# Two decode layers on one core: a ring of 4 KB loads made one stretch of 28 KB, with larger loads and two regions exchanged

## The chip, the cores and the metric

One core of one Trainium2 chip runs the whole program. The metric is device time in microseconds for one execution, median of repeated runs: 707.14 us before the change, 706.82 to 707.31 over three runs. All data is float32, so the bytes that come from memory are fixed: about 299 MB in one execution.

## The reference

Two identical layers are applied to four rows of 512 numbers (a decode step for a batch of 4). Each layer is attention over a cache and then a gated feed-forward, both with a layer norm in front and a residual behind:

```python
x = x + attention(layernorm(x), k_cache, v_cache, wq, wo)   # 32 query heads, 8 groups, 4096 keys of 128
x = x + (silu(layernorm(x) @ w1) * (layernorm(x) @ w3)) @ w2  # 512 -> 1792 -> 512
```

Both layers use the same caches and the same weights. The caches of K and V are 67 MB each, the weights together 28 MB, far more than fits on the chip, so the second layer reads nearly everything again; only wq, wo and V of the last group stay between the layers.

## The kernel before, in words

**Units.** One tile, `arena`, holds all data that comes from memory. It has 216 units of 1 KB in each of the 128 partitions (128 KB over all partitions). Loads are counted in these units: a group's K or V is 64 units (8192 KB), a piece of a weight is 3 or 4 units (384 or 512 KB).

**The list of loads.** Lines 105 to 151 write out, by hand, the order of all 95 loads of the arena as `plan` entries: the source, the keys that a load brings, and for some a fixed place. `pump` (line 156) goes down this list whenever space has come free, takes a place from `take` (line 55), and issues the load from SyncE's queue at line 163. Since the list is in order, a load that has to wait holds all that stand behind it. What a load waits for on the chip is that the last reader of the units that it overwrites has read them. `done` and `vacate` give units back as the matmuls that read them are written.

**The first layer.** The regions are wq in 0 to 64, wo in 64 to 128, and `KEPT` in 128 to 192, where V of group 7 (`TURN`) stays for both layers. Until wo and that V come, the 128 units from 64 to 192 hold one group's K and one group's V in turn. Group 0's K is loaded in two halves, and group 7's V in four parts of 32, 16, 8 and 8 units. The scores (line 371) multiply a query against K blocks of 8 units; `weigh` (line 414) multiplies the weights of the softmax against V blocks of 8 units.

**The ring.** During the first feed-forward nothing else is free, so its weights and the first half of the second layer's first K pass through a ring of seven slots of 4 units: one at 64 to 68, where wo's first piece (key 0) was, which is saved to PSUM by `stash` and put back by `restore`, and six at 192 to 216. The last two units, 214 to 216, otherwise hold the softmax weights `pT`. `piece` (line 116) makes the loads of the ring: four each of w1a, w3a (4 units), w1b, w3b (3 units), seven of w2 and seven halves of K blocks (4 units). `product` (line 474) multiplies with one key of w1 or w3, `down` (line 496) with two keys of w2 by `pair` (line 433). `busy` (line 257) issues matmuls whose result nobody reads, between the others.

**The turn.** Behind the ring, the second layer's queries are made (line 315), and each use of a wq key gives 8 units back. The first loads after the ring go there: one more half block, four blocks of 8 units of K of group 7, and K of group 6 in parts of 8, 8, 8, 8, 16 and 16 units. From then on K and V come in loads of 32 and 64 units until the last feed-forward, whose weights are loaded in parts of 16, 12, 8, 4 and 2 units.

```python
for i in range(7):
    piece("half", i, slots[i])
ring["to"] = len(plan) - 1
piece("half", 7, None)
cache("k", 1, TURN, (8,) * (NB - SPLIT), SPLIT)
```

Of the kernel before, what the change touches and what calls it, by code (L numbers as in the profile page):

```python
# [15 lines left out]
REP = HQ // HKV  # L16
P = 128
KC = D // P
NB = 8
# [13 lines left out]
SPLIT = 4  # L33
# [4 lines left out]
def tile_decode_layers(ctx: ExitStack, tc: tile.TileContext, x, kt, v, wq, wo, w1, w3, w2, out):  # L38
# [9 lines left out]
    WQ, WO, KEPT = 0, 64, 128  # L48


    PT = ARENA - 2
    free = [(WO, PT - WO)]
    ring = {"to": 0}

    def take(n, at=None):
        if at is not None and at < WO:
            return at
        for i, (lo, size) in enumerate(free):
            if at is None and state["next"] > ring["to"]:

                end = min(lo + size, PT)
                if lo < WO + 4 and end > WO:
                    if WO - lo >= n:
                        end = WO
                    else:
                        lo = WO + 4
                if end - lo < n:
                    continue
                a = lo
                lo, size = free[i]  # L70
            else:
                a = lo if at is None else at
            if lo <= a and a + n <= lo + size:
                free[i:i + 1] = [(p, s) for p, s in ((lo, a - lo), (a + n, lo + size - a - n)) if s]
                return a
        return None
# [30 lines left out]
    for n in range(HKV):  # L107
        cache("k", 0, n, (32, 32) if n == 0 else (64,))
        if n == 0:
            load(wq[:, 8 * KB:64 * KB], 8, [("wq", 0, g) for g in range(1, HKV)], WQ + 8)  # L110
        else:
            cache("v", 0, n - 1, (64,))
    cache("v", 0, TURN, (32, 16, 8, 8))
    weights("wo", wo, 0, (32, 16, 8, 4, 4), 4, WO)

    def piece(name, i, at):

        w, layer, lo, n, per = {"w1a": (w1, 0, 4 * i, 4, 4), "w3a": (w3, 0, 4 * i, 4, 4),
                                "w1b": (w1, 0, 16 + 3 * i, 3, 3), "w3b": (w3, 0, 16 + 3 * i, 3, 3),
                                "w2": (w2, 0, 4 * i, 4, 2), "half": (kt[TURN], 1, 4 * i, 4, 4)}[name]  # L120
        weights(name, w[:, lo * KB:(lo + n) * KB], layer, (n,), per, at, 2 * i if name == "w2" else i)

    RING = KEPT + 64
    slots = [WO] + [RING + 4 * i for i in (5, 4, 3, 2, 1, 0)]
    for i in range(4):
        piece("w1a", i, (slots[6], slots[1], slots[2], slots[3])[i])
    for i in range(4):
        piece("w3a", i, (slots[4], slots[5], slots[0], slots[6])[i])
    for i in range(4):
        piece("w1b", i, RING + 21 - 3 * i)  # L130
    for i in range(2):
        piece("w3b", i, RING + 9 - 3 * i)
    piece("w2", 0, slots[0])
    for i in range(2, 4):
        piece("w3b", i, RING + 9 - 3 * i)
    for i in range(1, 7):
        piece("w2", i, slots[i])
    for i in range(7):
        piece("half", i, slots[i])
# [16 lines left out]
    def pump():  # L156
        while state["next"] < len(plan):
# [7 lines left out]
            if i == 0:  # L165
                nc.sync.dma_start(xt[:8], x[:8])
# [23 lines left out]
    nc.scalar.dma_start(xt[8:], x[8:])  # L190
# [242 lines left out]
    def pair(i, left, w, first, last):  # L433

        for n in range(2):
            for e in range(2):
                r = 32 * (2 * n + (e ^ (i % 2)))
                nc.tensor.matmul(x_ps[r:r + B, e * 256:e * 256 + 256], left(2 * i + n), w(n)[:, e * 256:e * 256 + 256],
                                 start=first, stop=last)
# [11 lines left out]
    def restore():  # L451
        assert take(4, WO) == WO
# [3 lines left out]
    def project_o(layer, g, first=False, last=False):  # L456
        for i in range(2):
# [3 lines left out]
            if last or not layer and g == TURN - 1:  # L461
                pair(i, lambda h: oT[:, g, h, :], lambda j: w[:, j, :], False, last and i == 1)
# [7 lines left out]
    def feed_forward(layer, mean):  # L470
# [3 lines left out]
        def product(name, ps, lo, n, fill=keep, ks=range(KC)):  # L474
            for k in ks:
# [20 lines left out]
        def down(i):  # L496
            ws = [loaded("w2", layer, 2 * i + n) for n in range(2)]
            if keep:
                pair(i, lambda m: hT[:, m, :], lambda n: ws[n], i == 0, i == WT // 2 - 1)
            else:  # L500
                for n in range(2):
                    for k in range(KC):
                        nc.tensor.matmul(x_ps[32 * k:32 * k + B, 0:P], hT[:, 2 * i + n, :],  # L503
                                         ws[n][:, k * P:(k + 1) * P], start=False, stop=(i == WT // 2 - 1 and n == 1))
            for n in range(2):
                done("w2", layer, 2 * i + n)
# [130 lines left out]
```

## Time and profile before

| | before |
|---|---|
| median of 3 runs | 707.14 us |
| the profiled execution itself | 706.78 us |
| its span, first to last instruction | 705.0 us |
| PE busy | 400.1 us, 57% |
| DVE busy | 85.0 us, 12% |
| ACT busy | 38.3 us, 5% |
| SyncE's DMA queue, share of 16 engines | 99.1% |
| read from memory | 298.85 MB |
| loads into the arena | 95 |

The page comes from one execution. Shares of the span are averages over stages. The row of DMA digits gives the busy share of the 16 DMA engines in 40 slices of the span, and the row under it what they moved. A chain of waits, followed back from the last instruction, shows which work ended last at each step. The profiled execution took 1.78 us more than its span, for what lies around the first and last instruction, and 0.36 us less than the median.

### The profile page before, as it was taken

Reading aid. Unit: us, or ns where it says so; the run is one execution under the profiler, and the core shown is the slowest. Engines: PE = TensorE matmul, PEld = TensorE weight load, DVE = VectorE, ACT = ScalarE, POOL = GpSimd, SP = SyncE. Lnnn points to the kernel's source line nnn. Section 1 sums busy time; section 2 is a strip of 40 time slices with the busy share of each in tenths; the row PEclk is TensorE's granted clock in tenths of the full one; section 3 lists DMA queues with packets and bytes.
Section 4 is the critical chain, followed back from the end, with each engine's and each line's share of the span. In section 5 each row is a group of like instructions: output and inputs, shape, how many; then the busy total and the mean of one; then the engine's idle time right before and its main releaser. Section 6 shows DMA issues by size and latency. Waiting matters only on the chain. (4 is left out here: it accounts for less than half of the span.)

```text
span 705.0 us, 6895 instructions
## 1 busy us (share of the span) xinstructions
PE 400.1 (57%) x3082; PEld 132.1 (19%) x3082; DVE 85.0 (12%) x290; ACT 38.3 (5%) x87; POOL 2.9 (0%) x10
## 2 busy tenths in 40 slices
PE   4555454546555553547677894365563545467666
PEld 2111011111111120112143231011120111122224
DVE  2001010101011010101111111020010101010111
ACT  0000000000000000002001000000000000000101
POOL 0000000000000000000000000000000000000000
PEclk9766777777677787768899997587697878788899
DMA  9999999999999999999999999999999999999996
GB/s 387 461 403 472 414 417 436 450 417 431 455 416 432 435 436 420 442 421 423 413 404 406 416 438 438 446 424 421 461 421 424 440 439 421 431 432 419 426 425 270
DMA packets 14003, 299.35 MB, mean 425 GB/s; under 512 B 1687, under 2 KB 1815, under 8 KB 6551
## 3 DMA queue, kind: packets, MB, share of 16 engines
q1 hardware_dynamic: 13840, 298.92, 99.1%
q8 instruction: 24, 0.39, 0.2%
q10 hardware_dynamic: 135, 0.01, 0.0%
q14 instruction: 4, 0.03, 0.0%
HBM read 298.85 MB, written 0.07 MB: 424 GB/s over the span
## 5 line engine op out<-in xcount | busy, mean ns | idle before, releaser
L414 PE MATMUL o_ps<-arena 128*32 128x512 f32 x1024 | 145.7, 718 | 150.8 <-DMA arena<-in_v 137.6
L371 PE MATMUL s_ps<-arena,qpad 128*32 128x512 f32 x1024 | 152.1, 749 | 82.5 <-DMA arena<-in_kt 82.5
L414 PEld LDWEIGHTS o_ps<-arena 128*32 128x32 f32 x1024 | 37.3, 129 | 257.3 <-issue 224.5
L371 PEld LDWEIGHTS s_ps<-arena,qpad 128*32 128x32 f32 x1024 | 39.5, 133 | 177.7 <-issue 165.6
L423 DVE SCALAR_TENSOR_TENSOR p<-o_ps,parts,p 128x512 f32<-128x512 f32 x16 | 12.0, 750 | 270.9 <-PE o_ps L414 270.9
L378 DVE TENSOR_REDUCE top<-s_ps 128x1 f32<-128x512 f32 x16 | 11.0, 690 | 194.0 <-PE s_ps L371 194.0
L315 PE MATMUL o_ps<-arena,xpad 128*32 128x512 f32 x112 | 16.2, 707 | 10.5 <-DMA arena<-in_wq 10.5
L421 ACT ACTIVATE p<-o_ps,parts 128x512 f32<-128x512 f32 x16 | 11.0, 687 | 192.5 <-PE o_ps L414 184.6
L445 PE MATMUL x_ps<-arena,oT 128*4 128x512 f32 x104 | 14.1, 653 | 9.1 <-DMA arena<-in_wo 5.6
L402 PE MATMUL t_ps<-ident,p 128*128 128x128 f32 x64 | 11.2, 302 | 13.5 <-ACT p L396 13.5
L425 PE MATMUL t_ps<-ident,p 128*128 128x128 f32 x64 | 10.5, 287 | 14.3 <-DVE p L423 14.2
L389 ACT ACTIVATE f<-d 128x1 f32<-128x1 f32 x16 | 3.2, 203 | 256.3 <-DVE d L387 256.3
L396 ACT ACTIVATE p<-s_ps,top 128x512 f32<-128x512 f32 x16 | 10.9, 684 | 75.9 <-PE t_ps L425 75.9
L425 PEld LDWEIGHTS t_ps<-ident,p 128*128 128x128 f32 x64 | 6.7, 141 | 29.6 <-DVE p L423 29.6
L403 DVE COPY arena<-t_ps 128x512 f32<-128x512 f32 x16 | 11.1, 691 | 9.6 <-PE t_ps L402 9.6
L259 PE MATMUL m_ps<-ident,rows 128*32 128x128 f32 x70 | 11.9, 273 | 0.0
L402 PEld LDWEIGHTS t_ps<-ident,p 128*128 128x128 f32 x64 | 7.1, 147 | 22.2 <-ACT p L396 19.2
L478 PE MATMUL o_ps<-arena,xpad 128*32 128x192 f32 (+1 forms) x128 | 8.1, 360 | 2.9 <-DMA arena<-in_w 2.8
L478 PE MATMUL s_ps<-arena,xpad 128*32 128x192 f32 (+1 forms) x128 | 7.9, 359 | 2.3 <-DMA arena<-in_w 2.1
L259 PEld LDWEIGHTS m_ps<-ident,rows 128*32 128x32 f32 x70 | 7.5, 110 | 3.5
L315 PEld LDWEIGHTS o_ps<-arena,xpad 128*32 128x32 f32 x112 | 3.7, 126 | 20.7 <-DMA arena<-in_wq 11.6
L320 DVE COPY p<-o_ps 128x256 f32<-128x256 f32 x2 | 0.8, 424 | 44.9 <-PE o_ps L315 44.9
(97 smaller groups left out, 139.9 us busy)
## 6 DMA issues: line engine op xcount, KB each, us to landing
arena<-in_kt SPq DMA_DIRECT2D x4, 4096.0 KB, 20.1
arena<-in_v SPq DMA_DIRECT2D x4, 4096.0 KB, 33.0
arena<-in_w SPq DMA_DIRECT2D x17, 512.0 KB, 10.1
arena<-in_kt SPq DMA_DIRECT2D x8, 1024.0 KB, 9.8
arena<-in_wq SPq DMA_DIRECT2D x1, 7168.0 KB, 39.5
arena<-in_v SPq DMA_DIRECT2D x3, 2048.0 KB, 36.8
arena<-in_wo SPq DMA_DIRECT2D x1, 4096.0 KB, 25.5
arena<-in_kt SPq DMA_DIRECT2D x8, 512.0 KB, 8.2
```

Source lines behind the costliest of these rows:

```text
L259: nc.tensor.matmul(m_ps[turn["m"] ^ 1][0:32, 384:512], rows, ident, start=True, stop=True)
L315: nc.tensor.matmul(ps[32 * k:32 * k + 32, :], xpad[:, k, lo:lo + 32], w[:, k, :], start=first, stop=last)
L371: nc.tensor.matmul(s_ps[32 * b:32 * b + 32, :], qpad[:, b, lo:lo + 32], k[:, j, :], start=(blk == 0), stop=(blk == NB - 1))
L378: nc.vector.tensor_reduce(top[:, 0:1], s_ps, axis=AX.X, op=ALU.max, negate=True)
L402: nc.tensor.transpose(t_ps[:, i, :], p[:, i * P:(i + 1) * P], ident)
L403: nc.vector.tensor_copy(pT.rearrange("p i r -> p (i r)"), t_ps.rearrange("p i r -> p (i r)"))
L414: nc.tensor.matmul(o_ps[32 * b:32 * b + 32, :], pT[:, i, 32 * b:32 * b + 32], w[:, b, :], start=(i == 0), stop=(i == NI - 1))
L421: nc.scalar.activation(p, o_ps, AF.Copy, scale=st["parts"][:, 0:1])
L423: nc.vector.scalar_tensor_tensor(p, o_ps, st["parts"][:, 1:2], p, op0=ALU.mult, op1=ALU.add)
L425: nc.tensor.transpose(t_ps[:, j, :], p[:, j * P:(j + 1) * P], ident)
L445: nc.tensor.matmul(x_ps[r:r + B, :], left(2 * i + n), w(n), start=first, stop=False)
L478: nc.tensor.matmul(ps[32 * j:32 * j + 32, lo:lo + n], x32[:, k, :], w[:, j * n:(j + 1) * n], start=(k == 0), stop=(k == KC - 1))
```

## The change

The list of loads has 77 entries instead of 95. The regions KEPT and WO exchange places: KEPT is 64 to 128, WO 128 to 192. wo is laid out from the top down, with key 0 at the end of the first load, so that key 0's four units lie at 188 to 192 and join the units 192 to 216 to one ring of 28 units. The loads of the ring have 4, 6 or 8 units and lie at any offset in it. Three blocks of the second layer's first K come as halves (`SPLIT`), not four, as loads of 8, 4, 4, 4 and 4 units; behind the ring come 8, 16 and 16 units, and K of group 6 comes in four loads of 16. K of group 0 comes as one load of 64 units, V of group 7 as two of 32. `take` keeps new loads off the four units of wo's key 0 in the second layer, as before. `down` takes one key of w2 at a time (`half_product` issues half of `pair`'s matmuls), and no product with w2 stands between those with w3b any more. All 128 rows of x are loaded from ScalarE's queue, where 8 of them came from SyncE's. The order of wo's heads in memory changes to fit.

```diff
-SPLIT = 4
+SPLIT = 3
-    WQ, WO, KEPT = 0, 64, 128
+    WQ, KEPT, WO = 0, 64, 128
-    PT = ARENA - 2
-    free = [(WO, PT - WO)]
+    PT, RING = ARENA - 2, WO + 60
+    free = [(KEPT, PT - KEPT)]
...
+            at = WO if (which, layer, g) == ("k", 0, 0) else at
...
-        cache("k", 0, n, (32, 32) if n == 0 else (64,))
+        cache("k", 0, n, (64,))
...
-    cache("v", 0, TURN, (32, 16, 8, 8))
-    weights("wo", wo, 0, (32, 16, 8, 4, 4), 4, WO)
-    def piece(name, i, at):
...
+    cache("v", 0, TURN, (32, 32))
+    lo = 64
+    for first, n in ((None, 32), (8, 16), (12, 8), (14, 4), (15, 4)):
+        lo -= n
+        some = [*range(1, 8), 0] if first is None else range(first, first + n // 4)
+        r = 0 if first is None else 4 * first
+        load(wo[:, r * KB:(r + n) * KB], 4, [("wo", 0, i) for i in some], WO + lo)
+    for name, r, n, per, first, at in (
+            ("w1a", 0, 4, 4, 0, 4), ("w1a", 4, 4, 4, 1, 8), ("w1a", 8, 8, 4, 2, 12), ("w3a", 0, 8, 4, 0, 20),
+            ("w3a", 8, 4, 4, 2, 0), ("w3a", 12, 4, 4, 3, 4), ("w1b", 16, 6, 3, 0, 8), ("w1b", 22, 6, 3, 2, 14),
+            ("w3b", 16, 6, 3, 0, 20), ("w3b", 22, 6, 3, 2, 0), ("w2", 0, 8, 2, 0, 6), ("w2", 8, 6, 2, 4, 14),
+            ("w2", 14, 8, 2, 7, 20), ("w2", 22, 6, 2, 11, 0), ("half", 0, 8, 4, 0, 6), ("half", 8, 4, 4, 2, 14),
+            ("half", 12, 4, 4, 3, 18), ("half", 16, 4, 4, 4, 22), ("half", 20, 4, 4, 5, 0)):
+        w = {"w1": w1, "w3": w3, "w2": w2, "ha": kt[TURN]}[name[:2]]
+        weights(name, w[:, r * KB:(r + n) * KB], int(name == "half"), (n,), per, RING + at, first)
     ring["to"] = len(plan) - 1
-    piece("half", 7, None)
-    cache("k", 1, TURN, (8,) * (NB - SPLIT), SPLIT)
+    cache("k", 1, TURN, (8, 16, 16), SPLIT)
     for n in range(1, HKV):
-        cache("k", 1, order[1][n], {1: (8, 8, 8, 8, 16, 16), 2: (32, 32)}.get(n, (64,)))
+        cache("k", 1, order[1][n], {1: (16, 16, 16, 16), 2: (32, 32)}.get(n, (64,)))
...
-            if i == 0:
-                nc.sync.dma_start(xt[:8], x[:8])
...
-    nc.scalar.dma_start(xt[8:], x[8:])
+    nc.scalar.dma_start(xt, x)
...
-        product("w3b", o_ps, FA, FB, ks=range(0, 2))
-        if keep:
-            down(0)
-        product("w3b", o_ps, FA, FB, ks=range(2, KC))
+        product("w3b", o_ps, FA, FB)
...
-        for i in range(1 if keep else 0, WT // 2):
-            if i == (4 if keep else 0):
+        for m in range(WT):
+            if m == (8 if keep else 0):
                 tail_tiles()
-            down(i)
+            down(m)
```

## Rows read from the trace of the kernel before

**Rows 1.** The page: span, engines, DMA queues.

```profile
span 705.0 us, 6895 instructions
PE 400.1 (57%) x3082; PEld 132.1 (19%) x3082; DVE 85.0 (12%) x290; ACT 38.3 (5%) x87; POOL 2.9 (0%) x10
...
q1 hardware_dynamic: 13840, 298.92, 99.1%
q8 instruction: 24, 0.39, 0.2%
```

**Rows 2.** The chain that ended last, in order: start us, us, what.

```profile
446.82 33.26 DMA arena<-in_kt
...
488.67 30.10 DMA arena<-in_kt
...
526.80 32.19 DMA arena<-in_kt
...
567.38 30.31 DMA arena<-in_kt
...
701.37 0.45 PE x_ps L503 x8
```

**Rows 3.** Two stretches: us, busy by engine, granted clock, DMA share, GB/s.

```profile
350.00:400.00 50.00, 42.00 (x449) 18.92 (x445) 6.03 (x28) 4.07 (x10) 1.10 (x2) 1.00 1.02 407
430.00:440.00 10.00, 6.16 (x32) 1.50 (x32) 0.00 (x0) 0.00 (x0) 0.00 (x0) 0.66 1.02 437
```

**Rows 4.** Line 163, three single loads: start; the line below, us to landing.

```profile
L163 SPq DMA_DIRECT2D arena<-in_kt x1: 328/328/328, 376.4 to 376.4; - x1
DMA to landing us min/median/max: 8.2/8.2/8.2
...
L163 SPq DMA_DIRECT2D arena<-in_kt x1: 328/328/328, 386.0 to 386.0; - x1
DMA to landing us min/median/max: 6.2/6.2/6.2
...
L163 SPq DMA_DIRECT2D arena<-in_kt x1: 328/328/328, 395.8 to 395.8; - x1
DMA to landing us min/median/max: 16.3/16.3/16.3
```

**Rows 5.** PE in order of time, two starts on 3-unit loads: start, us, what.

```profile
367.36 0.53 PE L478 MATMUL s_ps<-arena,xpad 128*32 128x192 f32 x8 [0.18 <-DMA arena<-in_w]
...
369.29 0.53 PE L478 MATMUL s_ps<-arena,xpad 128*32 128x192 f32 x8 [0.22 <-DMA arena<-in_w]
```

**Rows 6.** PE in order of time, around the other merged loads.

```profile
24.99 6.45 PE L371 MATMUL s_ps<-arena,qpad 128*32 128x512 f32 x32 [3.48 <-DMA arena<-in_kt]
41.93 9.09 PE L315 MATMUL o_ps<-arena,xpad 128*32 128x512 f32 x56 [10.49 <-DMA arena<-in_wq]
...
320.40 3.64 PE L414 MATMUL o_ps<-arena 128*32 128x512 f32 x32 [0.86 <-ACT p L421]
...
334.34 3.64 PE L414 MATMUL o_ps<-arena 128*32 128x512 f32 x32 [1.21 <-ACT p L421]
...
345.17 1.88 PE L445 MATMUL x_ps<-arena,oT 128*4 128x512 f32 x7 [5.59 <-DMA arena<-in_wo]
```

**Rows 7.** PE in order of time, from the ring's end to the turn.

```profile
379.03 0.33 PE L538 MATMUL t_ps<-ident,p 128*128 128x128 f32 x1
...
379.91 0.61 PE L438 MATMUL x_ps<-arena,qT 128*4 128x256 f32 x8 [0.28 <-DVE qT L494]
...
380.85 0.61 PE L438 MATMUL x_ps<-arena,qT 128*4 128x256 f32 x8
...
382.13 0.61 PE L438 MATMUL x_ps<-arena,qT 128*4 128x256 f32 x8 [0.46 <-DMA arena<-in_w]
...
384.91 1.06 PE L315 MATMUL t_ps<-arena,xpad 128*32 128x512 f32 x8
```

**Rows 8.** Line 163, the first load of all: start; the line below, us to landing.

```profile
L163 SPq DMA_DIRECT2D arena<-in_wq x1: 368/368/368, 0.7 to 0.7; - x1
DMA to landing us min/median/max: 4.8/4.8/4.8
```

More of the change, by code (lines that the diff above doesn't have):

```diff
@@ L45, in tile_decode_layers @@
     arena = const.tile([P, ARENA * KB], F32, name="arena")
-    WQ, WO, KEPT = 0, 64, 128
-    PT = ARENA - 2
-    free = [(WO, PT - WO)]
+    WQ, KEPT, WO = 0, 64, 128
+    PT, RING = ARENA - 2, WO + 60
+    free = [(KEPT, PT - KEPT)]
     ring = {"to": 0}
     def take(n, at=None):
-        if at is not None and at < WO:
+        if at is not None and at < KEPT:
             return at
+        closed = state["next"] > ring["to"] and at is None
         for i, (lo, size) in enumerate(free):
[L59 to L75, printed above, removed]
+            parts = [(lo, RING), (RING + 4, PT)] if closed else [(lo, lo + size)]
+            for a, end in parts:
+                a, end = max(a, lo), min(end, lo + size)
+                a = a if at is None else at
+                if lo <= a and a + n <= end:
+                    free[i:i + 1] = [(p, s) for p, s in ((lo, a - lo), (a + n, lo + size - a - n)) if s]
+                    return a
         return None
@@ L431, in weigh, with half_product @@
         nc.vector.tensor_tensor(oT[:, g].rearrange("p h b -> p (h b)"), raw, st["r"], op=ALU.mult)
[L433 to L439, printed above, removed]
+    def half_product(m, left, w, first, last):
+        for e in range(2):
+            r = 32 * (2 * (m % 2) + (e ^ (m // 2 % 2)))
+            nc.tensor.matmul(x_ps[r:r + B, e * 256:e * 256 + 256], left, w[:, e * 256:e * 256 + 256], start=first, stop=last)
     def whole(i, left, w, first):
@@ L461, in project_o @@
             if last or not layer and g == TURN - 1:
-                pair(i, lambda h: oT[:, g, h, :], lambda j: w[:, j, :], False, last and i == 1)
+                for j in range(2):
+                    half_product(2 * i + j, oT[:, g, 2 * i + j, :], w[:, j, :], False, last and i == 1)
             else:
@@ L494, in tiles, with down @@
             nc.vector.tensor_copy(hT[:, 4 * lo:4 * lo + n, :], t_ps.rearrange("p i (j b) -> p (i j) b", j=4)[:, 4 * lo:4 * lo + n, 0:B])
-        def down(i):
-            ws = [loaded("w2", layer, 2 * i + n) for n in range(2)]
+        def down(m):
+            w = loaded("w2", layer, m)
             if keep:
-                pair(i, lambda m: hT[:, m, :], lambda n: ws[n], i == 0, i == WT // 2 - 1)
+                half_product(m, hT[:, m, :], w, m < 2, m >= WT - 2)
             else:
[L501 to L506, printed above, removed]
-            if keep and i < WT // 2 - 1:
+                for k in range(KC):
+                    nc.tensor.matmul(x_ps[32 * k:32 * k + B, 0:P], hT[:, m, :], w[:, k * P:(k + 1) * P],
+                                     start=False, stop=(m == WT - 1))
+            done("w2", layer, m)
+            if keep and m % 2 and m < WT - 1:
                 busy()
-            elif not keep and i in (1, 3):
+            elif not keep and m in (3, 7):
                 busy(3)
```

30 lines of the change are left out of this document (5 added, 25 removed).

## The prediction

> **What bounds the kernel now.** I read the page first, for who is busy, then the chain, for what ended last, then stretches and single loads, for what one load costs. On the page [rows 1] SyncE's DMA queue fills 99.1% of the 16 DMA engines' time, while PE is busy for 57% and no other engine for over 12%. The chain [rows 2] agrees: from 446 us on it alternates between a K load in flight and the few matmuls that free the space for a load after it, and each piece marked DMA spans 30 us because the load queued behind others, not because it is slow. So the end of the program is the end of a stream of loads that hardly ever pauses, plus PE's last 0.45 us and the store. The time can change in three ways only: the stream needs less time for the same bytes, the stream runs dry somewhere, or the tail behind the last byte changes. The last six loads, which feed the tail, keep their sizes and order, so I cost the tail at nothing.
>
> Is the stream equally fast everywhere? No [rows 3]: it moved 407 GB/s from 350 to 400 us, where loads of 3 and 4 units pass, and 437 GB/s from 430 to 440 us, where they have 32 units or more, at a DMA share of 1.02 in both. The engines are equally full, but small loads carry something besides bytes.
>
> **What one load costs besides its bytes.** Landings that follow one another in a full queue give the time per load. K loads of 64 units: the chain [rows 2] has landings at 480.08 (446.82 + 33.26), 518.77, 558.99 and 597.69, with a V load between each two, so a load takes 38.69 / 2 = 19.35 us, and again 38.70 / 2. Loads of 8 units: from 392.2 to 412.1 [rows 4] eight of them land, 2.49 us each. Loads of 4 units: from 384.6 to 392.2 there are six, 1.27 us each. Loads of 3 units: PE starts on them 1.93 us apart for two, 0.965 us each [rows 5]. Now the same 64 units by each size: 8 x 2.49 = 19.9 us, 0.55 us over 19.35 for 7 more loads, 0.08 each; 16 x 1.27 = 20.3 us, 0.95 for 15 more, 0.06 each; 21.3 x 0.965 = 20.6 us, 1.23 for 20.3 more, 0.06 each. A load in a full queue costs 0.06 to 0.08 us besides its bytes.
>
> **The change part by part.** It removes 18 loads: 1 of K of group 0, 2 of V of group 7, 1 each of w1a and w3a, 2 each of w1b and w3b, 3 of w2, 4 of the halves and K of group 7, 2 of K of group 6. 18 x 0.06 = 1.1 us, 18 x 0.08 = 1.4 us; I take 0.067, nearer to the small sizes where most of them are, so 1.2 us. As I find no row where the stream of the first layer or of the ring stands still, all of it lies on the path.
>
> The 18 issues that SyncE saves, 0.33 us each [rows 4], are worth nothing: the queue holds five and more microseconds of work at each. PE does the same matmuls, since `half_product` twice is `pair`.
>
> K of group 0 in one load: its first matmul starts where the second half's do now, at 24.99 us, and the whole needs twice the 6.45 us of a half, until 38 us. PE's next step waits for wq until 41.93 us [rows 6], so this hides, with 4 us to spare; and without that cover V of group 0 would still come in time, since K of group 1 takes the stream 19 us beyond wq. x from one queue: 8 rows move from SyncE's queue to ScalarE's, 0 to 0.1 us, and PE has nothing to do with q before 24.99 us; nothing.
>
> V of group 7 in two loads: PE starts its second half at 334.34 us, while the last parts are still coming, and is through at 337.98; later it waits 5.59 us for wo [rows 6]. Even a start at 337.98 us, when the last part must long have landed, delays it by 3.64 us only, inside that wait. wo's first load, which lands at about 345 us, will wait until PE has read all of group 6's V, at 324.04 (320.40 + 3.64), 21 us ahead of its landing and with V of group 7 queued in front of it: nothing.
>
> **The ring's new waits** are the term that can go wrong. A load of 8 units waits for two keys that have themselves come in one load, so each space comes free later, in steps of 2.5 us. I followed each load to the last reader of the units it overwrites and put landings at the new times. Within the ring each is issued 4 to 6 us ahead of its predecessor's landing; today that is 5 at the narrowest (386.0 us against 392.2 less 1.27 [rows 4]).
>
> The narrowest is the first load behind the ring, block 3 of K of group 7 (8 units), which waits for PE to read wq's first key of the second layer. That PE step comes after all of w2. Its predecessor, the last half block, lands at 389.7 us now (392.2 less two loads of 4) and will at 388.9, with 0.8 us saved by then. Before that come halves of 8, 4, 4, 4 and 4 units (7.6 us) and w2's last load of 6 (1.88 us, between 1.27 and 2.49), so w2's last three keys land at 381.3 us and the four before them at 379.4. PE then takes key 7 (0.3 us), the tiles (379.03 to 379.91 now, 0.88 us [rows 7]) and three pairs 0.94 us apart (379.91 to 380.85), and is done with w2 at 383.2 us, against 382.74 now. That is 0.45 us later; the chain from there to wq's first key keeps its length, and the issue goes from 386.0 to 386.45 us. The lead shrinks from 5.0 to 2.4 us. Behind it on SyncE's queue stand the two loads of 16 units of K of group 7; they wait for further wq keys, their leads come out a little wider by the same working, and PE's scores wait for all three.
>
> Which lead is needed, no row shows, since no load is ever issued so late. Bounds: the first load of all lands 4.8 us after its issue [rows 8] and needs 2.49 for its bytes, so 2.3 us of fixed time; what part of that lies behind the last byte, the predecessor's landing has too. So the lead needed is between 0 and 2.3 us, and 2.4 just clears the upper end. I cost it at nothing; if the sum of PE steps is 0.5 us longer than mine and the upper bound holds, it costs 0.4 us there and about as much at the next load.
>
> Behind the turn, scores of group 6 wait for 16 units at a time. The loads that then depend on them are issued well over 5 us ahead, and PE has less left when the last 16 units come than the 9.7 us that the next 32 take: nothing.
>
> **Sum.** 706.78 - 1.2 = 705.6 us for the profiled execution; it stood 0.36 us under the median of the runs, so 705.9 us against 707.14. That is 0.17% less, and a measurement of this kernel can tell about 0.2%, 1.4 us: the forecast is a small gain that counts as no change.
>
> **The rivals.**
> *The gain is larger.* At 0.08 us a load it is 1.44 us, 705.7. There is also a pause that I leave as it is: from 518.77 to 558.99 us the two loads took 40.22 and not 38.70 us [rows 2], 1.5 us more, and 24 packets of instructions go over the same engines [rows 1]. If one such pause fewer falls on the engine that is last, 704.4. For it: these costs add on the same engines. Against: the instruction count hardly changes.
>
> *Nothing is left of it.* The leads at the turn fall short by up to a microsecond at two loads, or the 0.06 us is not paid on the slowest engine: 706.2 to 708.5 us.
>
> *Slower: PE turns slow in the ring and the queue runs dry at the turn.* Today PE works at full clock through the ring (1.00 from 350 to 400 us, busy for 42 of 50 us, small waits between), while between 430 and 440 us, busy for 6.2 of 10 us on large loads, 0.66 is granted [rows 3]. With loads of 8 units PE gets its work in larger lumps with longer waits between. If the clock falls to the lower of its two levels (1.2 GHz) there, the 3.8 us of PE work from 382.13 to 385.97 us [rows 7] become about 7. The issue then comes at 389.6 us, 0.7 us after the predecessor's landing; with half of the upper bound needed as lead it is dry for 1.8 us, and the two loads behind lose about as much again each, as their wq steps slow too: 3.6 to 5.4 us lost, less 1.2, so 709.5 to 711.3. It decides from 2.6 us lost on. Against it: the fillers of `busy` stay in place and the waits in the ring grow only to about 1.2 us (2.49 less two products of 0.6). The Trainium skill, "TensorE: Matmul & The Clock Gate", section "HAM oscillation", speaks against the change here: a loop whose compute per tile is shorter than the wait for the next tile's DMA goes back to the low clock at every tile. By that rule this rival would be the likeliest; the row of 350 to 400 us, with a wait for DMA at every load and a clock of 1.00, does not bear it out so far.
>
> *A load's fixed time is paid in series.* The first load's 2.3 us [rows 8], 18 times, would be 41 us: 666 us. The 1.27 us between landings of 4 units [rows 4] exclude it nearly. The Trainium skill, "DMA: Bandwidth & Descriptors", section on the anatomy of one DMA, gives each DMA about 2.0 us of fixed cost, measured on GpSimd's path; an estimate from that page would be 36 us less, and the trace does not agree.
>
> **How the numbers follow.** The forecast, a gain of 0.9 to 1.4 us, gets 0.48; the larger gain 0.30; nothing left 0.10; slower through the clock 0.11; in series 0.01. Faster by over 0.2% is 0.31, within 0.2% is 0.58, slower 0.11. The range reaches down to 705.0, for most of the larger gain, and up to 707.9, for most of the case where nothing is left; the slow rival lies outside.
>
> **What would show it.** Right: 77 loads, fewer small packets, the 350 to 400 us stretch above 410 GB/s, landings of 6 units about 1.88 us apart, the load at the turn issued about 386.4 us with a lead over 2 us, and the same 38.7 us per pair afterwards, each some 1.2 us earlier. Wrong: a granted clock under 1.00 between 355 and 390 us, a landing interval over 3 us for the 8 units at the turn, or landings of K at 64 units no earlier than now.

## The result, and the profile after

| | before, same chip | after |
|---|---|---|
| median | 706.98 us (10 runs) | 708.48 us (10 runs) |
| lowest to highest | 706.68 to 707.31 | 707.24 to 712.05 |
| the profiled execution, its span | | 712.05 us, 710.3 us |

The kernel became slower: the ratio is 1.0029, interval 1.0018 to 1.0039. Not only the median moved: the times lie 4.8 us apart where those of before lie 0.6 apart. That narrow spread is partly luck of ten runs: in the longer series below the kernel before reaches 709 us too. The profiled execution was the slowest of the ten, so its losses are larger than the median's; what it shows is where time can be lost.

The page of the kernel after (span, engines, DMA queues), beside [rows 1]:

```profile
span 710.3 us, 6864 instructions
...
PE 405.0 (57%) x3082; PEld 137.8 (19%) x3082; DVE 85.3 (12%) x290; ACT 38.4 (5%) x87; POOL 2.9 (0%) x10
...
q1 hardware_dynamic: 11232, 298.91, 98.3%
```

There are 2,608 packets fewer for the same bytes, as the change says, but the queue is 98.3% full and no longer 99.1%: somewhere it stood empty. PE is busy 4.9 us longer with the same 3082 matmuls, so its clock was lower somewhere. Two stretches account for this. The first is the ring and the turn. Windows of the kernel after (us, busy PE, PEld, DVE, ACT, POOL with counts, granted clock, DMA share, GB/s), beside [rows 3]:

```profile
360.00:366.00 6.00, 6.00 (x48) 3.28 (x49) 0.98 (x5) 0.47 (x1) 0.55 (x1) 0.50 0.94 355
366.00:372.00 6.00, 4.70 (x72) 3.12 (x71) 1.00 (x3) 1.91 (x3) 0.00 (x0) 0.97 0.94 324
372.00:376.00 4.00, 1.85 (x31) 1.04 (x22) 0.42 (x1) 0.00 (x0) 0.00 (x0) 1.00 1.00 415
376.00:380.00 4.00, 3.65 (x33) 1.88 (x34) 0.00 (x0) 0.00 (x0) 0.00 (x0) 0.57 1.00 420
...
350.00:400.00 50.00, 43.73 (x445) 20.77 (x437) 6.13 (x28) 4.08 (x10) 1.10 (x2) 0.90 1.00 391
```

The first two of these stretches in the kernel before:

```profile
360.00:366.00 6.00, 4.29 (x52) 2.19 (x52) 0.89 (x5) 0.47 (x1) 0.56 (x1) 1.00 1.03 401
366.00:372.00 6.00, 4.90 (x68) 2.49 (x62) 1.00 (x3) 1.91 (x3) 0.00 (x0) 1.00 1.03 398
```

From 350 to 400 us 391 GB/s moved, where it was 407. Most of the loss lies between 360 and 372 us, and the clock stood at its lower level (1.2 GHz) for six microseconds just there, and again from 376 us. Four loads of the ring and the turn in the kernel after (the load's line is 146: start, and under it us to landing):

```profile
L146 SPq DMA_DIRECT2D arena<-in_w x1: 328/328/328, 365.1 to 365.1; - x1
...
DMA to landing us min/median/max: 6.1/6.1/6.1
...
L146 SPq DMA_DIRECT2D arena<-in_w x1: 328/328/328, 367.1 to 367.1; - x1
...
DMA to landing us min/median/max: 6.6/6.6/6.6
...
L146 SPq DMA_DIRECT2D arena<-in_kt x1: 328/328/328, 379.8 to 379.8; - x1
...
DMA to landing us min/median/max: 7.3/7.3/7.3
...
L146 SPq DMA_DIRECT2D arena<-in_kt x1: 328/328/328, 389.5 to 389.5; - x1
...
DMA to landing us min/median/max: 9.0/9.0/9.0
```

The two loads of w3b (6 units) landed at 371.2 and 373.7 us, 2.5 us apart, where 6 units take 1.88 in a full queue. I call such an excess a load's **lateness**: the time between two landings, less 0.06 us and 0.302 us for each unit (19.35 us for 64). The **lead** is how long before its predecessor's landing a load is issued. In this execution w1b's second load was late by 0.17 us, w3b's two (leads 3.7 and 4.2) by 0.60 and 0.59, the half block of 4 units issued at 379.8 (lead 5.1, behind a load with 3.9) by 0.87, and the first load of 16 units, issued at 389.5, by 0.17: 2.4 us. In the kernel before no load of the ring or the turn was late by more than 0.10.

PE in order of time, in the kernel after, shows where the clock fell:

```profile
357.71 1.07 PE L458 MATMUL s_ps<-arena,xpad 128*32 128x256 f32 x16
359.93 1.93 PE L458 MATMUL s_ps<-arena,xpad 128*32 128x256 f32 x16 [1.14 <-DMA arena<-in_w]
...
362.74 1.08 PE L458 MATMUL o_ps<-arena,xpad 128*32 128x256 f32 x8
```

Sixteen matmuls take 1.07 us at 357.71, and behind a wait of 1.14 us for a load of 8 units eight take 1.08.

The second stretch is the tail. From the chain that ended last, and from PE in order of time, both in the kernel after:

```profile
590.19 27.67 DMA arena<-in_v
...
631.56 46.28 DMA arena<-in_v
677.88 3.69 PE o_ps L395 x16
...
706.12 1.37 PE x_ps L482 x43
```

```profile
677.88 3.64 PE L395 MATMUL o_ps<-arena 128*32 128x512 f32 x16 [4.37 <-DMA arena<-in_v]
...
689.20 3.64 PE L458 MATMUL s_ps<-arena,xpad 128*32 128x256 f32 x32 [0.26 <-DVE xpad L282]
...
693.72 3.64 PE L458 MATMUL o_ps<-arena,xpad 128*32 128x256 f32 x32
```

The first of these products in the kernel before:

```profile
684.06 1.93 PE L478 MATMUL s_ps<-arena,xpad 128*32 128x256 f32 x32 [0.26 <-DVE xpad L301]
```

In [rows 2] the chain ends with a DMA and 0.45 us of PE. Here it leaves the DMA for good at 677.88; from there it is PE's, with short steps of DVE between. A product of 32 matmuls takes 3.64 us (1.93 in the kernel before) until about 697: behind the wait of 4.37 us for V the clock stayed low, with PE hardly idle. PE was late when the last bytes came. They came at 703.66 us (701.33 before), and the span ended 6.6 us later (3.7 before). So the 5.3 us more of this execution are **2.3 in the stream and 2.9 in the tail**.

The stream's 2.3 can be added up: 18 loads fewer, -1.1; lateness in ring and turn, +2.4; +1.3 because outside the ring four landings came about 1.4 us late (at 62.7, 335.2, 424.2 and 677.8 us), where the kernel before has three of that kind (62.7, 330.4 and 539.6); small deviations make up the rest, -0.3.

### The profile page after: what moved, and what is told of

Same layout as the page of the kernel before. It is cut to its first block, busy times and chain, and to the rows that moved or that the text cites. A ratio compares the mean times of both kernels' runs of the same rounds, so it can differ in the third digit from the quotient of the medians.

```text
span 710.3 us, 6864 instructions
## 1 busy us (share of the span) xinstructions
PE 405.0 (57%) x3082; PEld 137.8 (19%) x3082; DVE 85.3 (12%) x290; ACT 38.4 (5%) x87; POOL 2.9 (0%) x10
## 3 DMA queue, kind: packets, MB, share of 16 engines
q1 hardware_dynamic: 11232, 298.91, 98.3%
## 5 line engine op out<-in xcount | busy, mean ns | idle before, releaser
L395 PE MATMUL o_ps<-arena 128*32 128x512 f32 x1024 | 149.1, 732 | 152.2 <-DMA arena<-in_v 140.4
L352 PE MATMUL s_ps<-arena,qpad 128*32 128x512 f32 x1024 | 146.6, 728 | 89.7 <-DMA arena<-in_kt 89.7
L458 PE MATMUL o_ps<-arena,xpad 128*32 128x192 f32 (+1 forms) x128 | 11.6, 470 | 2.0 <-DMA arena<-in_w 2.0
L458 PE MATMUL s_ps<-arena,xpad 128*32 128x192 f32 (+1 forms) x128 | 10.6, 455 | 1.9 <-DMA arena<-in_w 1.6
L418 PE MATMUL x_ps<-arena,qT 128*4 128x256 f32 x56 | 6.7, 479 | 1.7 <-DMA arena<-in_w 1.3
```

The source lines that it names most:

```text
L352: nc.tensor.matmul(s_ps[32 * b:32 * b + 32, :], qpad[:, b, lo:lo + 32], k[:, j, :], start=(blk == 0), stop=(blk == NB - 1))
L395: nc.tensor.matmul(o_ps[32 * b:32 * b + 32, :], pT[:, i, 32 * b:32 * b + 32], w[:, b, :], start=(i == 0), stop=(i == NI - 1))
L458: nc.tensor.matmul(ps[32 * j:32 * j + 32, lo:lo + n], x32[:, k, :], w[:, j * n:(j + 1) * n], start=(k == 0), stop=(k == KC - 1))
```

## The experiments

Four theories stood at the start or came up later. **Clock** (A): PE's clock falls in the ring, the products take longer, the loads are issued too late. **Leads** (B and D): the larger loads wait for more work to be done, are issued later, and at any clock this is too late; D says why a lead of 2 to 4 us is too late, namely that the 16 DMA engines do not run dry together: the landing counts the last of them, so some are empty while the predecessor is still landing. **Tail** (C): the end comes late because the clock is low in the tail, whatever the stream does. Each run stands against the kernel before on the same chip: the first four kernels below share one series, the next four a second, the last three and the second execution of six halves a third. The intervals of the ratios reach some 0.7 us to either side. Only three of the experiments lie clear of the kernel before, all slower: fillers in the tail, seven halves, and large ring with small turn. The argument therefore leans on the landings in the profiled executions, one of each kernel and two of the changed one.

**The same kernel again.** No edit.

> The changed kernel once more, nothing edited. Theory A (PE's clock falls to its lower level in the ring, PE reads late, SyncE issues late, the DMA engines that are ahead run dry): about 708.5 us, 1.5 above the kernel before, single times spread over 707 to 712; the profile has a granted clock under 0.9 between 355 and 385 us and loads of 6 units more than 2.1 us apart, and the more of the one the more of the other. Theory B (leads in the ring are too short at any clock, or rows of 6 KB are slow in themselves): the same median, but slow landings of 6 units also where the clock is 1.00. Theory C (PE's clock falls in the last feed-forward, and the end comes up to 3 us after the last landing): the profile has 4 us or more from the last landing to the end of the span where the clock is low after 677 us, and 3.7 where it is not.

Measured: 707.82 us (706.52 to 710.91), before 707.1, ratio 1.0011 [0.9999, 1.0022]. The loss is smaller than the first time and no longer clear of noise, with the same wide spread. In this execution the clock stood at 1.00 from 360 to 372 us, and w3b's second load was late all the same, by 0.65, and at the turn the 8 units (lead 2.8) by 0.31, the first 16 (lead 3.4) by 0.84. The last byte landed at 702.2 us and the tail took 3.3: the tail is not what makes the usual execution slow. Rows of 6 KB are not slow in themselves, as B also had it: two loads of 6 units in the kernel after, with leads of 6.3 and 5.7 us, landed 1.89 and 1.88 us behind their predecessors.

**More fillers in the ring.** `busy`, the matmuls that nobody reads, issues three where a merged load ends, not one.

```diff
-                    busy()
+                    busy(3 if k % 2 and keep else 1)
+                elif keep and k == 1:
+                    busy(3)
...
-            if keep and m % 2 and m < WT - 1:
+            if keep and m in (3, 6, 10):
+                busy(2)
+            elif keep and m % 2 and m < WT - 1:
```

> The changed kernel with more fillers of PE in the first feed-forward, 3 for 1 at the end of each load and 3 after w1a's second key, so that PE has no long idle stretch there; no load is touched. Theory A: clock 1.00 from 350 to 395 us, loads of 6 units 1.88 and of 8 units 2.49 us apart, 1.0 to 2.5 us less than the changed kernel: 706.0 to 707.5. Theory B: the clock rises, the landings stay 2.1 to 2.5 us apart for 6 units, 708.5. Theory C alone: 708.5 with the whole excess behind the last landing.

Measured: 707.95 us (707.36 to 708.60), 1.0008 [0.9999, 1.0017]. The slowest executions are gone, and the quickest too. Windows, and three loads, of this kernel:

```profile
366.00:372.00 6.00, 4.97 (x71) 3.75 (x72) 0.61 (x2) 1.91 (x3) 0.00 (x0) 1.00 1.01 405
...
386.00:387.00 1.00, 1.00 (x14) 0.46 (x10) 0.39 (x2) 0.00 (x0) 0.00 (x0) 1.00 0.97 393
387.00:388.00 1.00, 1.00 (x12) 0.26 (x8) 0.28 (x4) 0.37 (x1) 0.51 (x1) 1.00 0.77 246
388.00:389.00 1.00, 1.00 (x11) 0.35 (x4) 0.24 (x1) 0.00 (x0) 0.04 (x1) 1.00 0.94 320
389.00:390.00 1.00, 1.00 (x11) 0.78 (x14) 0.17 (x1) 0.00 (x0) 0.00 (x0) 1.00 1.01 426
```

```profile
L146 SPq DMA_DIRECT2D arena<-in_kt x1: 332/332/332, 383.3 to 383.3; - x1
...
DMA to landing us min/median/max: 5.7/5.7/5.7
...
L146 SPq DMA_DIRECT2D arena<-in_kt x1: 328/328/328, 386.6 to 386.6; - x1
...
DMA to landing us min/median/max: 5.3/5.3/5.3
...
L146 SPq DMA_DIRECT2D arena<-in_kt x1: 328/328/328, 388.8 to 388.8; - x1
...
DMA to landing us min/median/max: 9.0/9.0/9.0
```

The last half block landed at 383.3 + 5.7 = 389.0 us, yet from 387 to 388 only 246 GB/s moved and the engines were 0.77 full: many had nothing left, a microsecond or two before that landing. The trace counts 16 completions for each load, and the last of them is its landing. Ten of this half block's lie between 387.2 and 387.9 us. The first of the 8 units' comes at 390.9, so their bytes, 2.48 us of them, began to move at about 388.4: ten engines were empty for 0.5 us and more. The 8 units were issued at 386.6, with a lead of 2.4, and were late by 0.35; the 16 units (388.8 + 9.0) were late by 1.01. All this at a clock of 1.00 from 366 us on; ahead of that the fillers had not held it (0.76 from 355 to 360 us). So the clock is not needed for the loss, and what D claims of the engines is seen.

**A ring of small loads.** The ring's 19 loads become 30 of 2 to 4 units; regions and turn stay (88 loads).

```diff
-            ("w1a", 0, 4, 4, 0, 4), ("w1a", 4, 4, 4, 1, 8), ("w1a", 8, 8, 4, 2, 12), ("w3a", 0, 8, 4, 0, 20),
+            ("w1a", 0, 4, 4, 0, 4), ("w1a", 4, 4, 4, 1, 8), ("w1a", 8, 4, 4, 2, 12), ("w1a", 12, 4, 4, 3, 16),
+            ("w3a", 0, 4, 4, 0, 20), ("w3a", 4, 4, 4, 1, 24), ("w3a", 8, 4, 4, 2, 0), ("w3a", 12, 4, 4, 3, 4),
...
```

> The changed kernel with the loads of the ring cut again to 2, 3 and 4 units, 88 loads, in the one stretch; the exchanged regions, the larger loads in front of the ring and behind it stay. Theories A and B both: the ring runs as before, landings 1.27 and 0.98 us apart, 7 loads fewer than before give 0.4 to 0.5 us: 706.5 against 707.0. If instead the loads at the turn lose the time: still 708 to 708.5. Theory C alone: 708 and the same spread as the changed kernel.

Measured: 706.69 us (706.31 to 708.52), 0.9996 [0.9987, 1.0005]. No load of the ring was late by over 0.15 us; at the turn one was, the first 16 units (lead 4.0) by 0.47. Against 707.82 us for the changed kernel in the same series the ring's loads had cost about a microsecond, though the single times overlap (706.52 to 710.91 and 706.31 to 708.52).

**Fillers in the tail.** `busy(8)` in the last wait for V of group 0, ahead of the tail.

```diff
+                if layer and g == 0 and f == 1 and i == 1:
+                    busy(8)
```

> The changed kernel with eight fillers of PE in the last wait for V of group 0 in the second layer, where PE sits idle for 3 to 4 us ahead of the last feed-forward; nothing else. Theory C: the clock stays 1.00 from 680 us on, the span ends 3.5 to 3.9 us after the last landing, the slowest times (709.5 and more) go, the median falls by 0.5 to 1.5 us to about 707.5. Theory A or B alone: the median stays within 0.5 us of the changed kernel's.

Measured: 708.57 us (707.03 to 710.18), 1.0018 [1.0008, 1.0029]. The profiled execution had a short tail of 3.3 us and was slow all the same, 709.31: w3b's loads were late by 0.37 and 1.26, the first load of halves by 0.78, and the 8 units at the turn (lead 2.9) by 1.88. The clock was 1.00 from 677 to 684 us, as C asks, but 0.69 from 684 to 690: the fillers did not hold it. C does not explain the median.

**Seven halves.** As in the kernel before, seven halves pass the ring and the eighth stands behind it; then 16 and 16 units (78 loads).

```diff
-SPLIT = 3
+SPLIT = 4
...
-    cache("k", 1, TURN, (8, 16, 16), SPLIT)
+    weights("half", kt[TURN][:, 28 * KB:32 * KB], 1, (4,), 4, None, 7)
+    cache("k", 1, TURN, (16, 16), SPLIT)
```

> The changed kernel with seven halves in the ring instead of six, as the kernel before has: 4 units more are asked for ahead of the turn; the other loads of the ring stay large. Theory D (the stream is dry on the DMA engines that are ahead whenever a load is issued less than about 5 us before its predecessor lands on the last engine; at the turn because the ring holds one half less, in the ring because of the large loads): the first load behind the ring is issued 3.5 to 4 us ahead instead of 2.4, the landings at the turn lose 0 to 0.5 us instead of 0.5 to 1.8, those in the ring lose as in the changed kernel; 0.5 to 1.0 us less than the changed kernel, 707.0 to 707.5. Theory A (the clock alone): no change, 707.8 to 708.5.

A miss: 708.26 us (707.02 to 710.37), 1.0015 [1.0005, 1.0025]. The first 16 units had a lead of 2.6 and were late by 2.49: the load waits for two wq keys, so the half won in front of it is lost again. The clock had a share here too (0.79 from 380 to 388 us).

**Small ring and seven halves.** Both edits above (89 loads).

> The changed kernel with the ring's loads cut again to 2, 3 and 4 units and with seven halves in it: both causes undone, 90 loads; regions, the larger loads in front of the ring and behind the turn stay. Theory D: no dry stretch between 355 and 405 us, 5 loads less than the kernel before, 0.3 to 0.4 us less than it: 706.5 to 706.8. Theory A: the same. If something else in the exchanged regions costs time: 707.2 or more.

A miss: 707.35 us (706.57 to 709.49), 1.0000 [0.9990, 1.0011]. This profiled execution was the slowest, with a tail of 5.5 us. Nothing in the ring was late by over 0.15 us, but the first 16 units (lead 4.0) were, by 1.63. Loads of 16 units at the turn have to go too.

**The kernel before with six halves.** The one edit made alone, the other way round: six halves in the ring and five blocks of 8 units behind it (94 loads).

```diff
-SPLIT = 4
+SPLIT = 3
...
-    for i in range(7):
+    for i in range(6):
...
-    piece("half", 7, None)
```

> The kernel before with one part of the change alone: six halves in the ring instead of seven, and five blocks of 8 units behind it. All loads of the ring keep 3 or 4 units. Theory D: the first load behind the ring is issued 2.5 to 3.5 us ahead instead of 5.0, some engines have nothing between its issue and its predecessor's landing, 0.3 to 1.0 us lost: 707.3 to 708.0. Theory A: the clock in the ring is 1.00 as before, nothing lost, 707.0.

Measured: 707.45 us (707.17 to 709.52), 1.0007 [0.9998, 1.0015], without the profiled execution, which took 1195.85 us with PE busy for 95% of it; the cause of that is not known. A second one:

> The kernel before with six halves in the ring instead of seven and five blocks of 8 units behind it, once more for its profile; timed before at 707.5. Theory D: the first load behind the ring is issued 2.5 to 4.0 us ahead and the loads at the turn are 0.3 to 1.0 us late in all; the small loads ahead of them are not late.

That execution took 709.71 us. In the ring nothing was late, at a clock of 1.00; at the turn the 8 units (lead 3.7) were on time, the next two late by 0.38 and 0.74. The last byte landed at 702.3; the rest is a tail of 5.6 us at the low clock. One half fewer, in small loads, costs about half a microsecond, which is not clear of noise.

**The kernel before without the ring's fillers.** `busy` is left out of the products of the first feed-forward, so that the clock falls while the loads stay small.

```diff
-                if fill:
-                    busy()
...
-            if keep and i < WT // 2 - 1:
-                busy()
-            elif not keep and i in (1, 3):
+            if not keep and i in (1, 3):
```

> The kernel before without the matmuls that fill PE's waits in the products of the first feed-forward; no load is touched and no result changes. Theory A: the clock falls to half in the ring, PE reads each load later by 0.6 us and more, SyncE issues later, 1 to 3 us lost: 708 to 710. Theory D: the clock falls too, but a load is lost only where its lead falls under 5 us; the narrowest lead now is 5.0 at the turn, so 0.5 to 1.5 us, with the ring's other loads at 1.27 and 0.98 us apart. If the clock in the ring matters to neither: 707.0.

Measured: 707.45 us (706.74 to 710.72), 1.0002 [0.9990, 1.0013]. Two windows of it:

```profile
367.00:380.00 13.00, 10.86 (x95) 2.71 (x95) 0.93 (x3) 1.91 (x3) 0.00 (x0) 0.53 1.03 401
380.00:392.00 12.00, 11.75 (x66) 4.96 (x66) 2.12 (x11) 0.85 (x3) 0.55 (x1) 0.51 0.93 344
```

At half the clock the ring still moved 401 GB/s: its leads of 5 to 7 us take the slower products. At the turn, where the leads shrink to 2.4, 1.9 and 3.4 us, three loads were late by 0.66, 0.43 and 1.67. These loads are those of the kernel before, at 4 and 8 units: a short lead is enough, without larger loads. The low clock cost nothing in the ring, where it left leads of 5 us and more; at the turn it cost by shortening them. The median is 0.5 us above before's, not clear of noise.

**Leads kept.** The regions exchanged, K of group 0 in one load, V of group 7 in two, K of group 6 in four and two merged loads of w1a and w3a stay, since their leads are over 5 us; everything else in ring and turn is small again, with seven halves and four blocks of 8 (89 loads).

```diff
-SPLIT = 3
+SPLIT = 4
...
-            ("w1a", 0, 4, 4, 0, 4), ("w1a", 4, 4, 4, 1, 8), ("w1a", 8, 8, 4, 2, 12), ("w3a", 0, 8, 4, 0, 20),
-            ("w3a", 8, 4, 4, 2, 0), ("w3a", 12, 4, 4, 3, 4), ("w1b", 16, 6, 3, 0, 8), ("w1b", 22, 6, 3, 2, 14),
+            ("w1a", 0, 4, 4, 0, 4), ("w1a", 4, 4, 4, 1, 8), ("w1a", 8, 8, 4, 2, 12),
+            ("w3a", 0, 8, 4, 0, 20), ("w3a", 8, 4, 4, 2, 0), ("w3a", 12, 4, 4, 3, 4),
+            ("w1b", 16, 3, 3, 0, 8), ("w1b", 19, 3, 3, 1, 11), ("w1b", 22, 3, 3, 2, 14), ("w1b", 25, 3, 3, 3, 17),
...
-    cache("k", 1, TURN, (8, 16, 16), SPLIT)
+    weights("half", kt[TURN][:, 28 * KB:32 * KB], 1, (4,), 4, None, 7)
+    cache("k", 1, TURN, (8, 8, 8, 8), SPLIT)
```

> The changed kernel with every load cut back to the size before wherever its lead was under 5 us: small loads from w1b on, seven halves, four blocks of 8 units at the turn. Kept are the exchanged regions and the larger loads with leads of 9 us and more (K of group 0, V of group 7, the 8 units of w1a and of w3a, the 16 units of K of group 6); 89 loads, 6 fewer than before. Theory D: no load after 355 us is later than its size asks by over 0.15 us, leads of 4.9 us or more as before, 0.4 us less than the kernel before: 706.4 to 706.8. If the exchanged regions cost something by themselves, or 16 units of K of group 6 do: 707.2 or more.

Measured: 706.34 us (706.07 to 708.16), before 706.87, ratio 0.9995 [0.9986, 1.0004]. The last byte landed at 701.0 us. The median is 0.5 us below before's, about what six loads at 0.06 to 0.08 us give; the interval includes 1, so a gain is likely and not proven. Two things were not as expected: the narrowest lead was 4.5 us, and one load was late, by 0.67 with a lead of 6.9. Only the last of its 16 completions was late, at 391.3 us, the others ended by 390.6; the last section has the likely cause, an instruction packet at 389.4 us.

**Leads kept, and fillers in the tail.** The last edit and that of the tail together.

> The same with the eight fillers in the last wait for V that the run on the tail had. Theory C for what spread is left: where the clock is low from 677 us to 694 us the end comes 5 to 6.6 us after the last landing instead of 3.3 to 3.7; with the fillers all times lie within 1 us, the median at 706.3 to 706.7, nothing over 708. If the spread comes from elsewhere, it stays as without the fillers.

Measured: 706.44 us (706.13 to 707.12), 0.9994 [0.9985, 1.0002]. No execution took over 707.12, where the kernel before reached 709.26 in the same series. Windows of the tail in this kernel:

```profile
677.00:684.00 7.00, 4.64 (x62) 2.90 (x62) 2.16 (x8) 0.48 (x2) 0.00 (x0) 1.00 1.00 427
684.00:690.00 6.00, 4.15 (x78) 2.65 (x73) 1.37 (x6) 0.47 (x1) 0.55 (x1) 1.00 1.00 421
690.00:697.00 7.00, 5.49 (x103) 3.83 (x93) 1.29 (x5) 1.91 (x3) 0.00 (x0) 1.00 1.00 407
```

The same three stretches in the kernel after:

```profile
677.00:684.00 7.00, 4.76 (x20) 1.31 (x20) 1.10 (x3) 0.00 (x0) 0.00 (x0) 0.50 1.00 427
684.00:690.00 6.00, 5.01 (x34) 3.01 (x38) 1.05 (x6) 0.48 (x2) 0.00 (x0) 0.50 0.99 420
690.00:697.00 7.00, 7.00 (x64) 3.47 (x60) 0.98 (x5) 0.48 (x1) 0.55 (x1) 0.50 1.00 415
```

And the first two in the kernel before, without these fillers:

```profile
677.00:684.00 7.00, 4.72 (x38) 2.00 (x30) 1.97 (x7) 0.47 (x2) 0.00 (x0) 0.84 1.00 423
684.00:690.00 6.00, 5.38 (x96) 3.44 (x100) 1.55 (x8) 0.47 (x1) 0.55 (x1) 1.00 1.00 423
```

With the clock at 1.00 the tail took 3.6 us, and the 5 to 7 us of the slowest executions did not come. That the fillers did it is not shown: with the same fillers the clock fell to 0.69 in the run on the tail, and without them it stood at 1.00 from 677 to 690 us in "ring fillers". Only one of 11 executions of "leads kept" took over 707.2 us without them, so they matter seldom; that is C's share.

**Large ring, small turn.** The converse of the small ring: the ring's larger loads with seven halves, and four blocks of 8 behind it (80 loads).

```diff
-SPLIT = 3
+SPLIT = 4
...
-    cache("k", 1, TURN, (8, 16, 16), SPLIT)
+    weights("half", kt[TURN][:, 28 * KB:32 * KB], 1, (4,), 4, None, 7)
+    cache("k", 1, TURN, (8, 8, 8, 8), SPLIT)
```

> The changed kernel with its large loads in the ring, but seven halves in it and four blocks of 8 units behind it, as before: the turn undone, the ring kept, 80 loads. Theory D: the loads at the turn lose nothing or up to 0.5 us (2.5 in the run with seven halves and 16 units, whose load of 16 units was issued 2.6 us ahead), those of w3b and of the halves in the ring still 0.4 to 1.3 us in all; 707.0 to 707.5. If the ring alone is the cause: as the changed kernel, 708.

A miss, slower than expected: 707.94 us (706.33 to 709.39), 1.0015 [1.0004, 1.0026]. A load of 6 units (lead 4.9) was late by 0.37, a half (3.7) by 0.43, and at the turn a block of 8 (lead 6.2, the one ahead of it 4.6) by 0.94. So the turn's small loads were not safe behind the large ring, and this kernel as a whole costs no less than the change did in its second series.

**All runs together.** Narrowest lead, and lateness in ring and turn (sum of all over 0.12 us), in the profiled execution; the medians against the kernel before, us. The lateness is that of one execution, the median that of 10 to 12:

| kernel | loads | narrowest lead | lateness | median less before's |
|---|---|---|---|---|
| before | 95 | 4.9 | 0.0 | |
| after, first and second series | 77 | 3.6, 2.8 | 2.4, 1.8 | +1.50, +0.72 |
| ring fillers | 77 | 2.4 | 2.2 | +0.85 |
| tail fillers | 77 | 2.9 | 4.6 | +1.47 |
| small ring | 88 | 3.7 | 0.6 | -0.41 |
| seven halves | 78 | 2.6 | 3.6 | +1.33 |
| small ring and seven halves | 89 | 4.0 | 1.9 | +0.42 |
| large ring, small turn | 80 | 3.7 | 1.7 | +1.07 |
| before, six halves | 94 | 3.7 | 1.1 | +0.52 |
| before, no fillers | 95 | 1.9 | 2.8 | +0.52 |
| leads kept | 89 | 4.5 | 0.7 | -0.53 |
| leads kept, tail fillers | 89 | 5.1 | 0.3 | -0.43 |

Over these 13 executions 395 loads land between 355 and 412 us. Of those with a lead under 3.5 us, 9 of 10 are late by more than 0.15, by 1.0 us on the average; from 3.5 to 4, 6 of 14, and in 13 of 14 the load or the one behind it; from 4 to 5, 11 of 51; from 5 to 7, 5 of 200; above, 1 of 120. It is no sharp threshold, but at about 5 us the loss nearly ends: of the six late loads above, three stand right behind a load with a lead under 5.

## Why the prediction was wrong

**What held.** A load in a full queue costs 0.06 to 0.08 us, or a little more: until w3a's last load, before the ring's leads grow short, the stream was 0.5 us ahead (364.86 against 365.36 us) with five loads fewer, and "leads kept" is 0.5 us quicker with six fewer, not clear of noise. So K of group 0, V of group 7, wo and x cost nothing that shows. Pairs of 64-unit loads still take 38.7 us: V landed at 617.86 (590.19 + 27.67) and 579.15, and the landing of K is the one between. They did not come 1.2 us earlier, though: in the kernel before this V landed at 617.05. The position of the load at the turn was right as well: 386.45 us and a lead of 2.4 were forecast, and with the clock at 1.00 it was issued at 386.6 with a lead of 2.4. That the two figures agree so well is partly luck: in "same again", without the added fillers, they were 386.4 and 2.8, and in the slow execution, whose predecessor was late itself, 387.3 and 3.6.

**The step that failed.** "So the lead needed is between 0 and 2.3 us, and 2.4 just clears the upper end. I cost it at nothing." I took the first load of all as the bound: 2.3 us from issue to landing, besides its bytes. That is the fixed time of a load, and the lead has to cover it from the moment an engine runs out of packets, not from the landing. The landing is that of the last of 16 engines; in "ring fillers" the queue was thinned out at 387 to 388 us, one to two microseconds before the landing at 389.0. Fixed time and spread together make it about 5 us, which is the narrowest lead that the kernel before has. The completions show the same sum. The first of the first load's came 4.35 us after its issue, 1.9 us more than its 2.48 of bytes; and the 16 of one load in the kernel before lie 3.4 us apart in the ring (352.95 to 356.38 for the first of w1a) and 2.9 at the turn (389.30 to 392.24), so that 4.8 to 5.3 us are needed for no engine to run dry. With that figure the loads within the ring, which I had followed to "4 to 6 us ahead" and set down as nothing too, were in part already short. By the medians these cost more than the turn: the small ring brought the time back from 707.82 to 706.69, and the small turn with the large ring brought nothing (707.94, with half of its lateness at the turn). The term that I put at nothing measured 2.4 and 1.8 us of lateness, ring and turn together, in the two profiled executions.

The leads of before, never under 4.9, were a warning. That no load was ever issued later was a fact without a price, and I bounded the price from one side with a load that had no predecessor.

**Nothing is left of it** (chance 0.10) named short leads at the turn as the loss, up to a microsecond at two loads, and 708.48 lies just inside its 706.2 to 708.5 us. For the turn this was right in kind and size: 0.31 and 0.84 us in "same again". It said nothing of the ring.

**The slower rival** (chance 0.11) had the place and the direction, and half of the mechanism. The clock did fall: 0.50 from 360 to 366 us and 0.57 from 376 to 380, behind waits of 1.14 and 1.31 us for the larger loads. But the queue runs short at a clock of 1.00 too ("ring fillers", 707.95), and at the low clock small loads lose nothing in the ring ("no fillers", 401 GB/s). The clock is a second cause on top of short leads, and a reason for the spread of times, since it falls in some executions and not in others. The price, 3.6 to 5.4 us, was one and a half to three times the 1.8 to 2.4 us of lateness. The Trainium skill, "TensorE: Matmul & The Clock Gate", section "HAM oscillation", had the rule: compute that is shorter than the wait for the next tile's DMA goes back to the low clock. For the ring after the change the trace agrees in one execution (0.50 from 360 to 366 us, behind a wait of 1.14 us and 1.07 us of matmuls) and not in the other (1.00 there, behind a wait of 1.17 us); the row of before at 1.00, by which I set it aside, was measured with waits of at most 0.64 us in the ring.

**The tail** I had costed at nothing, because its loads keep sizes and order. At the median that holds (3.3 us in "same again", 3.7 in before). In the slowest executions it does not: 6.6 us here and 5.3 to 5.6 in three others (small ring, small ring with seven halves, six halves), each with the clock low from 677 us to about 694 or later. In the two profiled executions with fillers in the tail it did not come (3.3 and 3.6 us), nor in seven without. Whether the change makes this more frequent is open: the kernel before has runs over 708 us as well (7 of 34 in the first series, besides one of 787.71), but none of them was profiled.

Open in part: why lateness shows in the landing, which the last engine sets, although it is the first engines that run dry. It often comes one load later, as if the engines changed places. The trace shows one part: behind a short lead single packets take longer, so an engine can lose more than its empty time. Of the 8 units issued at 386.6 in "ring fillers" 15 packets took 0.49 to 0.85 us, where the median for their size is 0.31; in w3b's loads of the kernel after one took 1.75, median 0.23. In the kernel before no packet of this queue took 0.9 us over the median for its size. Which engine became the last was not followed.

## What to carry to other kernels

A stream in a full queue like this one needs its loads issued some 5 us before the predecessor has landed: the fixed time of 2 us, and the 3 us by which its 16 engines lie apart. So read the narrowest lead that the kernel has now, and cost every lead below it as lost time. Merging loads saved 0.06 to 0.08 us each here, and makes the space of several keys come free at once and later: merge where the lead is long, and leave small what is issued at the last moment. Behind a wait of a microsecond on TensorE the clock fell in one execution and not in another; where it falls, it eats the lead of loads that the products release, so look at the clock beside the leads.

## What was not expected of the hardware

A low clock can last while PE is hardly idle: 0.50 from 684 to 697 us in the kernel after, with PE busy for 12.0 of 13 us.

Landings come some 1.4 us late three times in the kernel before and four in the kernel after, in a full queue and with leads of up to 40 us. One more of them in one execution than in another is as much as the whole change was meant to bring. Each has one packet of the instruction queue (q8 in [rows 1]) in its stretch, which passes the same 16 engines. For the landing at 62.7 us of the kernel before, from 41.9 us on (packets, MB, share):

```profile
q8 instruction: 1, 0.02, 0.3%
```

The completions show what it does. At 41.9 us the 16 of a load lie 0.4 us apart. At 62.7 us fifteen of them still do, and the last is 1.5 us behind: the packet, 16 KB at 46.2 us, held one engine. Each later packet of 16 KB up to 300 us holds one more engine by as much, and an engine that is behind stays behind. At 314.3 us eight completions are 1.5 us late and one, after a packet of 8 KB, 0.8. The landing moves only when a packet falls on an engine that is already last, as at 330.4 and 539.6 us. So the engines of a long stream drift apart, to 3.4 us in the ring, and the lead that it needs grows with this.
